# Seven-product W_o for two row blocks, two more nested down products, LayerNorm-2 statistics on ScalarE, and a new order table

## The chip, the cores and the metric

The kernel runs on one NeuronCore of one Trainium2 chip. The metric is the device time of one execution in microseconds (us), as the median of repeated runs. One execution was also taken with the hardware profiler. Its engines are called PE (TensorE), DVE (VectorE), ACT (ScalarE), POOL (GpSimd) and SP (SyncE, which here only issues DMAs).

## What is computed

A transformer block with adaptive LayerNorm: linear attention and a gated GELU feed-forward, on 2048 rows of 1024 features, F = 3584, in bfloat16.

```python
mod = (_silu(c) @ w_mod).reshape(c.shape[0], 6, 1, -1)   # sa, ca, ga, sb, cb, gb
h = _layernorm(x) * (1 + ca) + sa
x = x + ga * _A_ref(h, A_wqkv, A_wo)      # linear attention, then @ wo
h = _layernorm(x) * (1 + cb) + sb
x = x + gb * _B_ref(h, B_w_gate, B_w_up, B_w_down)
...
    qkv = (x @ wqkv) ...                  # 32 heads of 32
    pq, pk = phi(q), phi(k)
    kv = einsum('bhsd,bhse->bhde', pk, v); z = einsum('bhsd->bhd', pk)
    o = (pq @ kv) / (pq @ z + 1e-06)
    return o.reshape(B, S, D) @ wo
...
    return _gelu(x @ w_gate) * (x @ w_up) @ w_down
```

## The kernel before

**Tiling.** The 2048 rows are four blocks b of 512 rows (`TG`), two blocks make a group g of 1024 rows. `KD` = 8 chunks of 128 features, `KH` = 4 is half of them; `NPR` = 14 pairs of F chunks; `HB` = 256, `NW` = 512. SBUF is one tile `mem`, cut by hand: a ring or buffer is given by its offset in KB, and buffers of different phases share offsets. PSUM is eight banks, handed out by `Banks`.

**Phases, in program order.** `kvq_phase` (LayerNorm 1, then K, V and Q), `merge_phase` (the last Q products; the heads' KV matrices are multiplied into W_o, giving `Wp`, so that the attention output is one product of the normalised `pqT[b]` with `Wp`), `wo_phase`, then for each group `gate_up(g)` and `down_out(g)`.

**Half-size products.** Many of the big products are split into quadrants and done by seven half-size products instead of eight (Strassen's scheme in Winograd's form): DVE forms sums of the operands' quadrants (`h_sum`, `w_sum`, `h2_sums`, `wd_sums`), PE makes the seven products, and DVE and ACT combine them out of PSUM. `seven` (line 906) is the list of stages for row products: stage 1 copies P1 out by ACT, stages 2, 5 and 7 end in `comb` (a DVE addition of PSUM and a copied product), stage 6 in `direct`. Inside gate/up and down some of the seven are split in the same way once more; in the down stage these are called nested. There a plain product (`plain`, line 1649) is 4 row tiles x 14 matmuls of 512 columns, and a nested one (`nested`, line 1679) is 7 steps g1 to g7 of 2 x 7 matmuls of 256 columns.

**`wo_phase` (line 1371).** Sixteen row tiles tt of 128 rows, four to a block. `wo_tile` (line 1315) loads x, makes 2 x 8 matmuls of 512 columns into a pair of PSUM banks (line 1324), adds x by DVE and stores the sum x2 to DRAM from POOL's queue. `den_sums` and `den_mul` bring in the attention's denominators for the blocks to come. For the tiles of group 0 (tt < 8) LayerNorm 2 follows at once: `ln2_stats` takes the statistics by DVE (two `bn_stats` of 512 columns and a `bn_aggr`, lines 733 and 735) and the reciprocal root by ACT (Ln and Exp, lines 746 and 747); `ln2_xhat` normalises by DVE and stores to DRAM from POOL's queue; after the fourth and the eighth tile SP issues a DMA transpose that brings 512 rows back as h2 (`h2_load`, line 1259). `h2_mods` then scale and shift h2 chunk by chunk (ACT line 1302, DVE line 1304; the scale comes from line 1382), and `h2_steps` form the sums of its quadrants. The other eight tiles, tt 8 to 15, follow group 0's on PE while this happens. Group 1 is normalised later, by `late_norm` on ACT during `gate_up(0)`.

**`gate_up(g)` (line 1482).** 14 units n, alternately gate and up; each loads 1 MB of weights (line 1405), forms sums on DVE and makes seven products (line 1444; the nested ones at line 1455). `fill` is a list of DVE work (the next unit's sums; in group 0 also `wd_sums` for the down weights) that is recorded between the products.

**`down_out(g)` (line 1628).** Seven products named after their weights: b11, b21, t0, t1, b22, t2, t3. b21, t0 and b22 are nested (`NESTED`), the sums of their weights' quadrants lie in DRAM (`u_scr`, written by `wd_sums` in group 0); b11, t1, t2 and t3 are plain. `sub_sums` forms the nested products' sums of activations. b11's result P1 stays in PSUM banks 0 to 3, where t1, t2 and t3 add to it (`start=False`), and is copied to `p1v` by ACT (line 1754); the nested products use banks 4 to 7. `W_AT` gives the places of the weights: numbers n of 3.5 KB slots at 7 + 3.5 n KB, where gate/up's buffers also lie. `rest` loads x2, `finish` and the functions `..._out` apply the gate gb and add x2, `store` writes the output (in the last group from ACT's queue).

**Order.** No instruction is issued when the program calls it: all are recorded in a `Plan`. `order` (line 322) runs list schedules with estimated costs; PE's instructions keep the order of the program and the other engines' are sorted by due times (`aim` ties a load to a due time). `refine` (line 349) then applies a table of shifts to the sequence of each engine that has an entry:

```python
SHIFTS = {            # DVE, ACT, POOL, SP; "z5" stands for five zeros
...
        for e, text in SHIFTS.items():
...
            seqs[e] = [seqs[e][i + d] for i, d in enumerate(shifts)]
```

Each engine works through its own sequence in order. There is no entry for PE.

Of the kernel before, what the change touches and what calls it, by code (L numbers as in the profile page):

```python
# [19 lines left out]
SHIFTS = {  # L20
    "DVE": (
        "z1 7 8 -2 7 7 -2 -1 1 -7 4 -8 4 -8 -1 z1 -9 2 -1 -1 1 2 2 -3 2 4 1 1 2 2 2 2 2 -11 7 7 -11 16 16 -4 -2 -1 13 1 "
        "-5 -9 -3 -10 -2 -4 -2 -4 -2 -4 -3 -3 z2 2 z1 -2 3 -1 -1 -1 z2 1 -1 1 12 6 2 z1 12 -3 3 1 -9 -8 1 19 -2 18 -8 "
        "18 -3 z1 -3 -14 -1 5 1 1 -2 z1 1 1 1 6 17 -11 6 8 11 2 -4 -3 -2 z1 6 2 z1 -3 z1 3 3 -26 2 -35 18 -33 -1 9 6 6 "
        "-4 -2 5 6 35 -7 2 3 33 4 1 -9 8 1 1 2 28 2 3 -18 23 1 -6 z2 -28 -26 -24 -10 z1 -2 -5 -7 -2 -7 -2 -4 -7 7 -4 -6 "
        "-4 -4 -7 -4 -3 1 1 -2 4 1 3 4 2 3 -6 3 3 -6 2 -2 -11 2 -1 -1 3 44 -1 -3 1 -1 38 -5 -2 1 1 -4 1 -5 -5 1 -2 z1 "
        "-3 -7 -1 -3 3 -3 5 31 5 -3 5 -6 -9 -9 -5 5 -4 -9 -8 -5 2 4 -5 -5 -1 -1 -10 2 5 2 10 -3 -13 3 -13 4 -6 -5 3 3 3 "
        "4 -7 1 -10 -8 z1 10 3 5 z1 -4 6 6 9 -7 -4 4 -9 -4 z1 5 -9 -7 -2 -1 -1 z1 2 -1 -1 z1 2 z1 1 -3 z3 2 2 3 12 9 7 "
        "3 -1 z1 7 1 -11 -2 1 -13 -8 4 4 4 -15 -3 -2 -4 z2 5 2 -1 -3 z1 -3 4 1 3 -2 -4 -2 1 -1 3 4 5 1 -4 -4 -4 -1 1 1 "
        "1 -3 1 1 1 1 1 1 1 8 3 4 4 -1 -4 -1 -5 1 2 2 4 -19 1 3 3 4 -1 1 -9 2 2 -9 -2 2 5 6 1 -1 -4 -1 -7 2 -2 -1 3 1 "  # L30
        "-2 -2 2 -1 10 -2 z4 5 7 -2 -1 3 -2 3 -12 -7 2 2 -5 1 -3 3 z1 -2 2 2 6 2 -3 2 -2 -1 1 20 z1 1 3 4 z1 -4 z1 2 5 "
        "7 -7 12 -2 -1 -6 -4 -2 -2 2 -2 -2 4 7 -1 7 -36 -2 52 -1 -3 26 31 -4 z2 17 -15 -1 -8 -2 -5 40 -1 -5 11 25 -3 "
        "-15 -3 -3 -2 32 -13 35 -12 30 -16 -4 -4 z1 8 -3 -12 -19 -15 10 -5 -20 5 -4 -1 -5 -12 4 2 -11 -4 16 -11 -5 z1 "
        "-24 9 1 17 1 1 2 8 -26 -19 -13 3 29 z1 30 6 26 28 -17 -3 2 -51 1 -14 26 1 -7 -2 -1 24 -2 -14 -21 -2 13 13 -12 "
        "-7 -3 -5 -11 -23 37 38 17 -2 -13 10 -9 13 -13 -2 19 20 1 -1 9 -6 -6 -1 z1 -15 34 -25 16 -6 z2 15 9 -1 -1 -32 "
        "-10 -18 27 1 18 -46 25 19 20 -46 1 -12 -3 -22 -19 -2 37 -5 -3 -16 -2 -20 25 32 -8 -1 -1 -10 33 28 -16 -10 18 "
        "z1 18 36 -2 14 -18 -37 -13 -11 -1 -11 34 -6 -4 -7 -5 -4 -1 -5 12 -9 4 -7 3 -1 -22 11 29 -24 23 -44 4 z1 1 -1 "
        "-5 z1 7 -17 1 -13 -39 z1 -38 -3 -16 z1 4 2 30 20 21 -9 28 3 -16 -8 -4 -4 1 11 -14 4 4 20 17 3 10 12 4 -8 -12 2 "
        "-24 4 z1 7 -22 7 -14 12 -13 8 -22 2 -27 -23 4 6 8 -1 2 -28 6 4 5 -9 -1 7 -11 8 -6 8 9 -28 -2 11 8 12 -7 6 -10 "
        "12 6 21 7 -10 24 26 4 1 11 3 -9 -13 -7 z1 2 -24 9 16 18 24 6 8 17 -8 10 5 -6 10 -34 11 11 -13 -36 16 -20 -3 6 "  # L40
        "13 -17 -4 4 -3 10 3 1 10 2 -47 -25 9 -33 5 10 -6 13 15 -2 -33 1 6 9 27 1 8 10 -38 10 5 5 6 10 -11 5 -16 9 11 "
        "-8 7 z1 3 7 10 -16 10 -5 -4 10 10 7 11 11 11 11 12 -9 -44 -43 12 z2 -10 6 9 5 z1 1 7 3 -44 13 5 1 8 3 -53 6 "
        "-27 -3 6 -27 -3 5 -28 z1 -6 7 2 2 5 7 -5 -4 13 -3 7 -4 7 19 2 -20 18 -7 -7 -5 5 12 15 -8 3 -12 3 12 13 -1 -8 "
        "-1 -12 -15 10 -12 26 3 7 -13 6 11 -18 -7 -1 2 11 -16 -13 14 4 7 13 11 5 30 30 3 29 29 30 z1 4 8 -16 -10 1 1 2 "
        "4 -17 -2 z1 2 4 14 -2 -1 2 -2 -1 z1 -31 -1 9 -35 5 -4 -39 5 6 -7 z1 2 -56 12 12 z1 1 2 -58 11 -4 2 13 20 10 6 "
        "6 -7 -10 -55 -1 5 -11 z1 11 -7 2 -10 8 -17 4 -1 -18 8 -3 8 14 -10 -6 5 -11 -1 z1 8 2 8 19 -10 -1 6 7 -3 4 5 12 "
        "5 -11 10 -4 -20 2 8 11 -25 -15 5 6 -8 3 -8 6 -19 6 8 10 -1 9 10 -15 -11 9 -17 1 -4 7 13 6 1 13 -14 -8 4 -15 6 "
        "-14 12 -6 11 -1 5 6 -7 11 -17 -1 -3 -13 8 -3 10 -1 -1 z1 4 6 13 14 -21 -18 -1 15 4 -1 z1 2 8 -10 7 3 z1 7 1 4 "
        "-6 -12 4 4 -26 4 -25 -16 3 -1 5 2 4 7 10 8 -6 z1 1 -14 2 6 -1 -11 7 5 -12 -9 6 3 3 -3 6 3 1 12 1 4 11 -14 z1 2 "
        "6 3 8 z1 9 7 9 19 -24 -1 -23 6 4 -13 8 -18 -7 -6 5 -17 1 9 7 -5 1 -11 10 -8 z1 6 -10 7 10 -9 -7 -1 8 -4 7 -8 6 "  # L50
        "9 11 -6 -1 2 3 7 7 10 7 -12 -1 9 4 -7 4 -5 7 7 8 2 -30 6 z1 2 -5 7 7 2 3 12 12 -17 -4 -3 4 10 8 10 11 9 -5 -2 "
        "-5 8 8 -11 8 -48 -12 6 10 6 -2 11 12 -9 -58 -4 10 -3 3 6 -22 -2 5 5 -4 -2 -10 7 2 2 5 -2 7 -32 8 -18 2 -5 5 6 "
        "10 -4 5 14 -11 -5 3 -11 -7 9 10 2 7 9 -8 6 10 7 -10 6 -16 10 -8 11 -13 10 12 -15 9 4 -2 5 7 7 17 7 9 7 9 10 "
        "-13 2 -19 -2 -29 -15 -17 -15 -32 -3 8 5 8 -1 z1 -7 5 -4 6 6 6 -11 z1 5 -7 -10 6 -8 14 8 -3 8 -9 8 z1 -2 -7 -6 "
        "z1 6 -4 13 -2 z2 -10 2 9 -2 -19 -3 -2 -1 -1 5 -2 5 -7 6 7 -3 -3 z1 5 5 -5 5 -12 -3 -6 -3 -1 2 2 2 2 2 -5 -5 z3 "
        "6 2 2 -3 -3 -3 2 2 -1 -4 z6 "
    ),
    "ACT": (
        "z1 2 2 -2 -2 1 1 -2 z1 1 1 -2 2 z1 -2 3 4 4 4 4 4 5 3 4 4 -8 3 3 3 3 3 -16 3 1 3 1 2 2 -22 2 3 -1 2 2 -2 -26 "
        "z2 2 -1 1 2 -3 2 z1 -3 z1 2 z1 2 z1 -4 1 -1 z1 1 -1 z3 1 1 -2 z2 2 -1 -1 5 1 1 -3 -3 1 -2 z3 1 -1 z2 2 2 -2 -2 "  # L60
        "z3 2 -1 -1 2 z1 -2 z2 1 2 -2 -1 z1 2 -1 -1 1 -1 z4 2 -1 -1 z1 1 -1 z1 1 1 1 -3 z1 1 -1 z3 1 -1 1 1 1 -3 1 -1 1 "
        "-1 1 1 -2 z1 1 1 1 -3 z7 2 2 -2 -2 z6 2 -1 1 -2 3 z1 3 -3 z1 -3 z2 2 3 1 2 -3 1 -6 z1 29 30 -1 -1 -1 -1 -6 -1 "
        "-3 z1 1 -3 z2 1 3 -6 2 2 3 3 -5 -1 1 -7 1 -1 1 16 -2 2 2 -25 1 -4 1 18 1 -1 -4 -1 -1 -1 25 -2 -2 -1 4 z1 -3 2 "
        "-1 1 -6 8 z2 -43 z1 -2 -1 z1 1 1 1 -5 -17 z1 -2 1 -1 z1 1 1 -2 z1 2 z1 2 -3 -1 z5 1 -1 2 7 18 -3 2 2 3 -6 -4 2 "
        "-7 2 -2 1 2 2 2 2 -13 3 1 2 2 4 1 3 3 3 -2 3 1 2 2 2 -19 1 1 2 -26 1 1 -3 1 -1 z1 1 2 3 1 2 4 6 4 6 4 6 4 -5 4 "
        "4 5 3 -17 4 -17 3 z1 3 4 2 3 -2 3 5 3 -1 -23 3 3 z1 2 -5 1 2 -29 2 z1 1 2 2 3 -2 2 4 2 4 4 4 4 4 -16 3 3 3 4 "
        "-13 1 3 3 3 -15 -2 2 3 1 -17 1 1 1 -6 z1 1 -1 3 1 3 4 z1 3 5 6 4 -8 4 4 4 -3 3 3 3 4 -12 -19 z1 2 2 2 -2 2 3 1 "
        "3 1 2 2 -6 -24 2 -1 3 1 5 6 6 -4 -1 6 z1 5 5 8 8 8 9 9 -17 -13 -2 14 -3 7 -11 12 10 z1 12 9 9 12 2 -9 -6 -6 8 "
# [315 lines left out]
def kernel(  # L384
# [224 lines left out]
    for at_x2, n in ((191, 4), (176, 4), (136, 2)):  # L609
        x2_ring.slots += Ring(at_x2, [D], BF16, n).slots  # L610
# [1273 lines left out]
```

## Time and profile before

| | us |
|---|---|
| median of 3 runs (lowest, highest) | 743.55 (743.28, 744.94) |
| the profiled execution, its own time | 743.69 |
| its span, first to last instruction | 741.9 |

| stage | from | to | PE's work in it |
|---|---|---|---|
| LayerNorm 1, K, V, Q, merge | 0 | 187.9 | first rows transposed from 8.6, continuous from 16.9 |
| W_o | 187.9 | 245.1 | 256 matmuls of line 1324 |
| gate/up, group 0 | 245.1 | 411.9 | lines 1444 and 1455 |
| down, group 0 | 411.9 | 492.6 | lines 1656 and 1700 |
| gate/up, group 1 | 492.6 | 657.4 | lines 1444 and 1455 |
| down, group 1 | 657.4 | 738.5 | lines 1656 and 1700 |
| last additions and stores | 738.5 | 741.9 | none |

The stages are read from the chain of waits, which follows the work that ended last back to its start; 85% of the chain is PE. The whole program is one long row of matmuls with a start of 16.9 us and a tail of 3.4 us. How full the other engines are is read stage by stage, not from the sums over the span.

### The profile page before, as it was taken

Reading aid. Unit: us, or ns where it says so; the run is one execution under the profiler, and the core shown is the slowest. Engines: PE = TensorE matmul, PEld = TensorE weight load, DVE = VectorE, ACT = ScalarE, POOL = GpSimd, SP = SyncE. Lnnn points to the kernel's source line nnn. Section 1 sums busy time; section 2 is a strip of 40 time slices with the busy share of each in tenths; the row PEclk is TensorE's granted clock in tenths of the full one; section 3 lists DMA queues with packets and bytes.
Section 4 is the critical chain, followed back from the end, with each engine's and each line's share of the span. In section 5 each row is a group of like instructions: output and inputs, shape, how many; then the busy total and the mean of one; then the engine's idle time right before and its main releaser. Section 6 shows DMA issues by size and latency. Waiting matters only on the chain.

```text
span 741.9 us, 11731 instructions
## 1 busy us (share of the span) xinstructions
PE 726.5 (98%) x4242; PEld 396.1 (53%) x4242; DVE 626.3 (84%) x1386; ACT 422.8 (57%) x772; POOL 96.7 (13%) x171
## 2 busy tenths in 40 slices
PE   4999999999999999999999999999999999999997
PEld 2444445444444455555555586545555555548664
DVE  6899978778896999999997798977788799778784
ACT  2575675769412888999867550026776767732000
POOL 1345634100031011220200000001000000000000
PEclk9999999999999999999999999999999999999999
DMA  9998798897799737565775897545231322488643
GB/s 307 330 305 227 111 185 156 312 367 236 190 282 281 249 103 228 194 215 188 260 180 168 245 284 252 204 151 188 68 114 57 115 71 100 143 232 268 205 171 101
DMA packets 141723, 149.15 MB, mean 201 GB/s; under 512 B 33760, under 2 KB 121312, under 8 KB 140384
## 3 DMA queue, kind: packets, MB, share of 16 engines
q1 hardware_dynamic: 125408, 116.14, 51.4%
q0 software_dynamic: 13904, 30.15, 14.1%
q10 hardware_dynamic: 2352, 2.10, 0.9%
q8 instruction: 33, 0.54, 0.3%
q14 instruction: 26, 0.21, 0.1%
HBM read 116.00 MB, written 32.37 MB: 200 GB/s over the span
## 4 chain that ended last, share of the span: by engine, by line
PE 85%; DVE 7%; ACT 4%; issue 2%; DMA 1%; SPq 0%; DVEq 0%; ACTq 0%
PE psum L1444 26%; PE psum L1656 13%; PE psum L1455 9%; PE psum L958 8%; PE psum L1324 7%; PE psum L1028 7%; PE psum L1700 6%; DVE mem L655 5%; PE psum L1057 4%; PE psum L782 2%; ACT mem L903 2%; PE psum L1072 1%; DMA mem<-in_w_mod_dram 1%; DVE psum L655 1%; ACT mem L1281 1%
## 5 line engine op out<-in xcount | busy, mean ns | idle before, releaser
L655 DVE TENSOR_TENSOR mem<-mem 128x512 f16<-128x512 f16 (+13 forms) x753 | 336.6, 488 | 15.2 <-ACT mem L1302 4.1
L1444 PE MATMUL psum<-mem 128*128 128x512 f16 x1144 | 282.3, 379 | 0.6 <-ACT psum L1500 0.2
L903 ACT ACTIVATE mem<-psum 128x512 f32<-128x512 f32 (+3 forms) x310 | 161.0, 550 | 112.4 <-PE psum L1700 45.5
L655 DVE TENSOR_TENSOR mem<-psum,mem 128x512 f16<-128x512 f32 (+4 forms) x204 | 155.0, 765 | 36.8 <-PE psum L1656 10.1
L1444 PEld LDWEIGHTS <-mem 128*128 128x128 f16 (+1 forms) x1144 | 111.8, 98 | 91.4 <-issue 1.6
L1455 PE MATMUL psum<-mem 128*128 128x256 f16 x742 | 115.9, 272 | 0.7 <-DVE psum L655 0.7
L1455 PEld LDWEIGHTS <-mem 128*128 128x128 f16 (+1 forms) x742 | 72.5, 98 | 55.9 <-issue 2.7
L1656 PE MATMUL psum<-mem 128*128 128x512 f16 (+2 forms) x462 | 99.2, 373 | 0.5 <-DVE mem L655 0.5
L655 DVE TENSOR_TENSOR psum<-psum,mem 128x256 f32<-128x256 f32 x106 | 45.5, 430 | 32.4 <-ACT mem L903 31.6
L1656 PEld LDWEIGHTS <-mem 128*128 128x128 f16 x462 | 45.2, 98 | 49.9 <-issue 0.7
L1700 PE MATMUL psum<-mem 128*128 128x256 f16 (+1 forms) x588 | 66.3, 273 | 0.1
L958 PE MATMUL psum<-mem 128*128 128x512 f16 (+1 forms) x280 | 62.7, 379 | 0.0
L1700 PEld LDWEIGHTS <-mem 128*128 128x128 f16 x588 | 57.5, 98 | 9.5 <-issue 0.2
L1500 ACT ACTIVATE psum<-psum 128x512 f32<-128x512 f32 x56 | 32.6, 582 | 48.4 <-PE psum L1444 28.8
L1324 PE MATMUL psum<-mem 128*128 128x512 f16 x256 | 55.9, 379 | 0.0
L1028 PE MATMUL psum<-mem 128*128 128x512 f16 x224 | 51.0, 379 | 0.0
L958 PEld LDWEIGHTS <-mem 128*128 128x128 f16 x280 | 27.0, 98 | 31.5 <-DVE mem L879 0.5
L1324 PEld LDWEIGHTS <-mem 128*128 128x128 bf16 x256 | 24.8, 98 | 30.4 <-issue 0.4
L1028 PEld LDWEIGHTS <-mem 128*128 128x128 f16 (+1 forms) x224 | 21.6, 98 | 26.7 <-issue 1.6
L1527 ACT ACTIVATE mem<-mem 128x512 f16<-128x512 f16 x56 | 34.6, 627 | 2.0 <-DVE mem L655 2.0
L1517 ACT ACTIVATE mem<-psum 128x512 f16<-128x512 f32 x56 | 33.1, 600 | 2.1 <-PE psum L1444 2.0
L733 DVE BATCH_NORM_STATS2 mem<-mem 128x6 f32<-128x512 bf16 x48 | 31.2, 676 | 1.8 <-DMA mem<-in_A_x_dram 1.7
(126 smaller groups left out, 519.5 us busy)
## 6 DMA issues: line engine op xcount, KB each, us to landing
mem<-in_B_w_gate_dram SPq DMA_DIRECT2D x14, 1024.0 KB, 5.4
mem<-in_B_w_up_dram SPq DMA_DIRECT2D x14, 1024.0 KB, 5.6
mem<-in_w_mod_dram SPq DMA_DIRECT2D x24, 512.0 KB, 6.9
mem<-us SPq DMA_DIRECT2D x24, 448.0 KB, 6.2
mem<-ts SPq DMA_DIRECT2D x6, 1792.0 KB, 7.9
mem<-in_A_x_dram SPq DMA_DIRECT2D x32, 256.0 KB, 6.4
ts<-in_B_w_down_dram POOLq DMA_DIRECT2D x28, 256.0 KB, 6.5
us<-mem POOLq DMA_DIRECT2D x7, 768.0 KB, 4.8
```

Of the source, the lines that this page charges most:

```text
L655: ve.tensor_tensor(out=out, in0=a, in1=b, op=op)
L903: ac.activation(out=t, in_=ps, func=AF.Copy)
L958: te.matmul(ps, lhsT=A[:, k, i * P:(i + 1) * P], rhs=B[:, k, :], start=(start and k == 0), stop=(k == KH - 1), skip_group_check=True)
L1028: te.matmul(o, lhsT=W[:, k, (j0 + i) * P:(j0 + i + 1) * P], rhs=h_form(a, k), start=(start and k == 0), stop=(k == KH - 1), skip_group_che ...
L1324: te.matmul(psw[:, half, :], lhsT=pqT[b][:, g, tl * P:(tl + 1) * P], rhs=Wp[:, g, half * NW:(half + 1) * NW], start=(g == 0), stop=(g == K ...
L1444: te.matmul(ps, lhsT=a[:, k, e, :], rhs=b[:, k, :], start=(start and k == 0), stop=(k == KH - 1), skip_group_check=True)
L1455: te.matmul(ps, lhsT=self.x[a][:, k, :], rhs=self.y[y][:, k, :], start=(start and k == 0), stop=(k == KH // 2 - 1), skip_group_check=True)
L1500: ac.activation(out=z, in_=x, func=AF.Copy)
L1517: ac.activation(out=o, in_=ps, func=AF.Gelu_apprx_tanh)
L1527: ac.activation(out=o, in_=o, func=AF.Gelu_apprx_tanh)
L1656: te.matmul(psm[:, q, c], lhsT=A[:, i, q * P:(q + 1) * P], rhs=wt[:, i, c], start=(start and i == 0), stop=(i == NPR - 1), skip_group_chec ...
L1700: te.matmul(ps[:, q, :], lhsT=a[:, k, q * P:(q + 1) * P], rhs=y[:, k, :], start=(start and q == 0 and k == 0), stop=(k == NPR // 2 - 1), s ...
```

## The change

- **W_o of blocks 2 and 3.** Tiles 8 to 15 are replaced by `wo_stages(2)` and `wo_stages(3)`, each the stages of `seven` with `pqT[b]` and `Wp` split into quadrants. `w_sum` forms the sums over `Wp` (8 DVE instructions), `wo_sum` those over `pqT[b]` (4 per block). x is loaded in two loads of 512 KB per block, and x2 stored in two.
- **Place.** The two blocks' stages are interleaved, and the last two stages of block 3 are handed to `gate_up(0)`, which runs them behind its first eight matmuls.
- **LayerNorm-2 statistics of group 0** are taken by ACT: a copy and a square with accumulated sums, then Ln and Exp; DVE's `bn_stats` and `bn_aggr` go.
- **Down, group 1.** b11 and t2 become nested. Their weights' sums are formed during `gate_up(1)` by `wd_later` (7 chunks of 8 DVE additions of 256 columns, two loads of 256 KB, one store of 512 KB) and kept in `v_scr`. P1 is now put together by `p1_quads` and copied into banks 0 to 3 by ACT; t2's finish `c22_quads` also prepares what t3's finish `c21_last` adds. `W_AT` has new places for group 1.
- **Buffers** for all this are placed at offsets that other phases use.
- **The table** `SHIFTS` is new for every engine and has an entry for PE as well; its numbers are left out below.

```diff
 SHIFTS = {
+    "PE": (
...
-    for at_x2, n in ((191, 4), (176, 4), (136, 2)):
-        x2_ring.slots += Ring(at_x2, [D], BF16, n).slots
+    x2_ring.slots += Ring(136, [D], BF16, 2).slots
+    x2p_rings = {2: Ring(176, [2, D], BF16, 2), 3: Ring(191, [2, D], BF16, 2)}
+    WpT = [at(o, [KH, NW], F16) for o in (40, 152, 184)]
+    Sp = {b: [at(o + 2 * i, [KH, HB], BF16) for i in range(3)] for b, o in ((2, 34), (3, 44))}
+    wf_ring = Ring(140, [2, NW], FP32, 3)
...
+    LATER = ("b11", "t2")
...
+    def wd_later(c):
+
+        u, steps = wdw_ring(), []
+        for j, name in enumerate(LATER):
+            raw = wdv_rings[name]()
+            sy.dma_start(out=raw, in_=wd_full[name][:, 2 * c:2 * c + 2, :])
+            q11, q12, q21, q22 = (raw[:, e, h * HB:(h + 1) * HB] for e in range(2) for h in range(2))
+            o0, o1, o2, o3 = (u[:, j, f, :] for f in range(4))
+            steps += [(o0, q11, q12), (o2, q12, q22), (o1, o0, q22), (o3, o1, q21)]
+
+        def last():
+            tt_op(*steps[-1], ALU.add)
+            gp.dma_start(out=v_scr[:, c], in_=u)
 
         return [lambda st=st: tt_op(*st, ALU.add) for st in steps[:-1]] + [last]
...
-    def ln2_stats(x2, rstd_of):
-        mv = ln_stats(x2)
-        return mv, rstd_of(mv)
+    def ln2_stats(x2):
+        nmean, rstd = sum_ring(), rstd_ring()
+        ac.activation(out=junk2, in_=x2, func=AF.Copy, scale=-1.0 / D, accum_out=nmean)
+        ac.activation(out=junk2, in_=x2, func=AF.Square, bias=nmean, accum_out=rstd)
+        ac.activation(out=rstd, in_=rstd, func=AF.Ln, bias=eps5, scale=1.0 / D)
+        ac.activation(out=rstd, in_=rstd, func=AF.Exp, scale=-0.5)
+        return nmean, rstd
...
+    def wo_stages(b):
+
+        xs = {}
+        for r in range(2):
+            xs[r] = x2p_rings[b]()
+            o = b * TG + r * HB
+            plan.ahead = 36000
+            sy.dma_start(out=xs[r], in_=x_in[o:o + HB, :].rearrange("(q p) n -> p q n", p=P))
+            plan.ahead = 14000
...
+        def comb(ps, sb, row, col, parts=1):
+            t = wt_ring()
+            add_parts(t, ps, sb, parts)
+            tt_op(dst(row, col), t, dst(row, col), ALU.add)
+            if (row, col) == (0, 1):
+                store(0)
+
+        def direct(ps):
+            tt_op(dst(1, 0), ps, dst(1, 0), ALU.add)
+            store(1)
+
+        return seven(mm, comb, direct, *((QC, QD) if b == 2 else (QA, QB)), ring=wf_ring)
...
-        for tt in range(NTT):
+        for tt in range(2 * TT):
...
+            ln2_xhat(tt, xt, *ln2_stats(xt))
+            if tt in (2, 3, 4):
+                for half in range(2):
+                    w_sum(Wp, WpT, (0, 1, 3)[tt - 2], half)
+            if tt == 5:
+                for j in range(4):
+                    wo_sum(2, j)
+        for half in range(2):
+            w_sum(Wp, WpT, 2, half)
+        for j in range(4):
+            wo_sum(3, j)
+        s2, s3 = wo_stages(2), wo_stages(3)
+        stages = [*s2[:5], s3[0], s2[5], s3[1], s2[6], *s3[2:5]]
+        for i, f in enumerate(stages):
+            f()
...
+            for m in {3: h2_mods[0][0], 7: h2_mods[0][1], 9: h2_steps}.get(i, ()):
+                m()
...
+        return s3[5:]
...
-    def gate_up(g):
+    def gate_up(g, before=()):
...
         for e in range(2):
             mm_k(X[e], w["a11"], e, h["b11"], True)
             seed(Z[e], X[e])
+        for f in before:
+            f()
...
+            if g and n < NPR // 2:
+                fill += wd_later(n)
...
+        def p1_quads(r, c, ps, sb, op):
+            if sb is None:
+                ac.activation(out=quad(p1v, r, c), in_=ps, func=AF.Copy)
+            else:
+                tt_op(quad(p1v, r, c), ps, sb, op)
+            if (r, c) in ((1, 0), (0, 1)):
+                for q in (2 * r, 2 * r + 1):
+                    ac.activation(out=psm[:, q, :], in_=p1v[:, q, :], func=AF.Copy)
...
+        def c22_quads(x2, x1):
+            def out(r, c, ps, sb, op):
+                t, d = f16_pair(), quad(p5v, r, c)
+                if sb is not None:
+                    tt_op(sb, ps, sb, op)
+                    ps = sb
+                tt_op(t, d, ps, ALU.subtract)
+                tt_op(d, ps, gate2(0, c), ALU.mult)
+                tt_op(t, t, gate2(1, c), ALU.mult)
+                tt_op(quad(x2, r, c), t, quad(x2, r, c), ALU.add)
+                if (r, c) in ((1, 0), (0, 1)):
+                    store(x2, 1, 1, 2 * r, 2 * r + 2)
+                tt_op(d, d, quad(x1, r, c), ALU.add)
+            return out
...
+        def c21_last(xt):
+            def out(q, ps, c):
+                t = c0_ring()[:, c]
+                tt_op(t, ps, gbrow[:, c], ALU.mult)
+                tt_op(xt[:, q, c], t, p5v[:, q, c], ALU.add)
+                store(xt, 1, 0, q, q + 1, c)
+            return out
...
-        run(*plain("b11", A11, p1_out, True))
+        if last:
+            sub_sums(A11, sub_c[:3], sub_c[3], [slice(0, 4), slice(4, NPR // 2 - 1), slice(NPR // 2 - 1, NPR // 2)])
+            run(*nested("b11", A11, sub_c[:3], sub_c[3], p1_quads))
+        else:
+            run(*plain("b11", A11, p1_out, True))
...
+        if last:
+            sub_sums(A21, sub_a, None, [slice(0, NPR // 2)])
+            x2, x1 = rest(1, 1), rest(1, 0, last_x)
+            n7 = nested("t2", A21, sub_a, None, c22_quads(x2, x1))
+            run(n7[0], n3[5], n7[1], n3[6], *n7[2:])
+            run(*plain("t3", A22, c21_last(x1), False))
...
-    wo_phase(merge_phase(kvq_phase()))
-    gate_up(0)
+    gate_up(0, wo_phase(merge_phase(kvq_phase())))
```

## The prediction

> **What bounds the kernel now.** I read the head of the page first, then the chain of waits, then the busy time by stage, then the groups of VectorE (DVE) instructions with shapes kept apart. Durations come from the profiled execution: span 741.9 us, its own time 743.69, so 1.8 us lie around the span. The runs shown have a median of 743.55, 0.14 below the profiled one. I therefore take differences from the span and apply them to 743.55.
>
> ```profile
> span 741.9 us, 11731 instructions
> PE 726.5 (98%) x4242; PEld 396.1 (53%) x4242; DVE 626.3 (84%) x1386; ACT 422.8 (57%) x772; POOL 96.7 (13%) x171
> ```
>
> TensorE (PE) is busy nearly throughout, but "busy" contains modelled ends, so it has to be checked by counting. The chain of waits gives the pace of uninterrupted runs of matmuls:
>
> ```profile
> 192.66 17.37 PE psum L1324 x80
> 210.12 31.10 PE psum L1324 x144
> 241.65 3.45 PE psum L1324 x16
> ...
> 657.37 12.09 PE psum L1656 x56
> 669.46 18.34 PE psum L1700 x168
> ```
>
> Each line is start, length, line and count. A 512-column matmul takes 31.10/144 = 0.216 us, a 256-column one 18.34/168 = 0.109 us. With these two prices the W_o stage, gate/up and down are filled: gate/up of group 0 has 576 and 364 matmuls, 124.3 + 39.8 = 164.1 us of its 166.8; of group 1, 568 and 378, 163.9 of 164.8. Thus PE could lose at most 2.8 + 0.9 us of waiting there. A matmul removed between 17 us and 738 us shortens the kernel by its price, as long as nothing else becomes late. What could is DVE:
>
> ```profile
> 187.90:245.10 57.20, 57.20 (x279) 25.60 (x280) 48.20 (x80) 17.24 (x35) 11.50 (x21) 1.00 0.96 263
> 245.10:411.90 166.80, 165.75 (x942) 91.78 (x940) 156.29 (x401) 140.55 (x286) 21.43 (x34) 1.00 0.61 195
> 411.90:492.60 80.70, 80.63 (x520) 50.63 (x518) 68.87 (x124) 20.05 (x32) 2.87 (x4) 1.00 0.76 239
> 492.60:657.40 164.80, 164.54 (x948) 92.52 (x946) 132.16 (x327) 116.36 (x246) 2.84 (x4) 1.00 0.35 112
> 657.40:738.50 81.10, 80.58 (x532) 51.82 (x530) 62.06 (x106) 9.62 (x17) 0.00 (x0) 1.00 0.63 202
> ```
>
> Columns: stretch, length, then busy time of PE, weight loads, DVE, ScalarE (ACT), POOL, then clock, DMA share, GB/s. The rows are W_o, gate/up and down of group 0, gate/up and down of group 1. DVE is idle for 9.0, 10.5, 11.8, 32.6 and 19.0 us in them: everywhere second, but close.
>
> The Trainium skill's page "Perfetto Trace Analysis" (Identifying the Most-Contended Engine) says matmul busy time is a poor measure and weight-load busy time a good one. By that, 53% would leave TensorE nearly half free and cutting matmuls would bring nothing. The trace has a weight load at 98 ns under a 216 or a 109 ns pace, so its share follows the matmul's width; I go by the pace.
>
> **W_o by seven products.** Row blocks 2 and 3 were 8 tiles of 16 matmuls; now each block is 7 products x 2 halves x 4 = 56 instead of 64. 16 x 0.216 = **-3.45 us** of PE. Cover: DVE. It loses, for tiles 0 to 7, two statistics of 0.673 and one aggregate of 0.199 each (8 x 1.545 = -12.4), and 8 additions of 1.214 (-9.7). It gains 8 sums over Wp and 8 over the transposed rows at 0.69 (+11.0), and per block two combinations at 1.22 + 0.69, one at 0.69 + 0.69 + 0.69 and one direct 1.22, together 7.1 (+14.2). Net +3.1 us, half of it ahead of the path's need: during tiles 0 to 7, where DVE had been full, it is relieved by 12.4 and gets 6 sums over Wp and 4 over block 2 (6.9). ACT gains per tile a copy 1.064, a square 1.145 and two accumulator reads 0.207 + 0.194 (8 x 2.61 = 20.9) and 6.5 of PSUM copies; it is idle for 40 of 57 us there, so that costs nothing. The chain of one tile grows by 2.61 - 1.545 = 1.1 us. What queues behind the new ACT wait on the tile's addition is the next tile's statistics and the modulation of h2, nothing of PE's until block 2's first copy.
>
> **The junction into gate/up.** Tile 7 ends on PE at 210.12 + 32 x 0.216 = 217.0 in both kernels. Behind it lay 128 matmuls and two small ones (to 245.1); now 112. The first 8 gate products are placed ahead of the last 16 of W_o, so they start near 238.2 and not at 245.1; the first product that needs the second half of h2 moves from 246.8 to about 243.4, 3.4 us earlier. What it needs:
>
> ```profile
> 235.69 8.57 ACT L1302 ACTIVATE mem<-mem 128x512 f16<-128x512 f16 x12 [13.44 <-DVE mem L1382]
> ```
>
> ACT stood idle for 13.4 us before this modulation, for one 0.16 us DVE instruction placed late, so the first half's eight can move ahead. The second half follows tile 7: store on POOL at 223.3 to 224.4, second transpose out of SP by 233.6, and with DVE relieved this starts a little earlier, less the 1.1 us. I have room for about 3 us against 3.4 wanted. But 16 DVE sums (7.7 us) follow there without a gap. Bounds 0 (cover holds) and +3.45 (all that W_o gave is waited away); I take **+0.5**, nearer zero because both the relief and the idle 13.4 us are rows.
>
> **Two more nested products.** b11 and t2 of group 1: 56 matmuls of 0.216 = 12.09 become 98 of 0.109 = 10.70: 2 x 1.39 = **-2.78 us** of PE. The pace is that of the nested products already there. Added around it:
> Gate/up of group 1 gets 56 DVE sums of 0.286 (16.0 us, less where they overlap) into 32.6 us of idle, 14 loads on SP, which has one big load per unit there, and 7 stores on POOL (busy 2.84 of 164.8). 26.2 of the 32.6 us are waits of an in-order queue for ACT copies (the group that adds into PSUM, 54 times). If none of them could be filled, 6.4 us would be left and 16.0 - 6.4 = 9.6 us would come on top; if the queue is ordered so that a sum stands ahead of each such wait, nothing does. Bounds 0 and +9.6; I take 0, since nothing needs these sums before 657 and DVE's order is made anew with them in it.
> Down of group 1 gets on DVE the sums over A11 (4 x (0.69 + 0.42 + 0.29) = 5.6, of which only the last 4 x 0.29 must wait for gate/up's end), over A21 (4 x 1.09 = 4.4), three combinations of P1 (2.1), a longer finish for t2 (per quadrant 2.9, and 0.69 in three: 13.7 for 6.1, +7.6), and 0.27 in each last addition (+1.1): 20.8 us by durations. With the 62.1 there now that is 82.9 in a stage of 81.1 - 2.8 = 78.3: 4.6 too many. It fits only if the 4.4 of A11 run in gate/up, which had 16 us left after the 56 sums, and because instructions overlap a little (two of 0.69 take 1.28). SP issues 14 loads for 2, some 1.2 us each, and DMA carries 2.7 MB more beside 16.6; the first seven can go before 657, where the DMA share is 0.57. Bounds 0 and the overflow worked out under the rivals; I take **+0.5**, nearer zero because 8.7 us of DVE's idle time lie between 720 and 738.5, where half of the longer t2 finish falls.
> The tail keeps its form; its last addition reads f32 instead of f16: 0.42 for 0.29, **+0.1**.
>
> **The shift table.** All queues are reordered, PE's for the first time. The gain is bounded by PE's waits: 3.7 us in gate/up and about 1 us at 16 us; the loss by group 0's gate/up, which loses 2.8 under the table of now. I take **-0.8**.
>
> Sum: -3.45 + 0.5 - 2.78 + 0.5 + 0.1 - 0.8 = -5.9 us. 743.55 - 5.9 = **737.6 us**, span near 736.0.
>
> **Rivals.**
> *Junction wait.* The transpose and the modulation can't come earlier, PE waits out W_o's gain. For it: tile 7 ends no earlier, DMA share is 0.96 there. Against: the rows above. 743.55 - 2.78 = 740.8 (the other small terms cancel).
> The Trainium skill's page "TensorE: Matmul & The Clock Gate" (The HAM clock gate) says an idle window of about 3.4 us halves TensorE's clock until it has worked as long again; by this the rival would cost an estimated 1.7 us more, 742.5. The trace has 512-column matmuls at 634 ns around 9 to 15 us, after the idle start, and 379 later, though the clock column shows 1.00.
> *DVE becomes the bound in the last down stage* (slower). Place: 657 to 720, where DVE idles 3.1 + 7.2 = 10.3 us. If the table lets nothing run early, 5.6 + 2.1 + 4.4 and half of the 7.6, 15.9 us, fall into it: 5.6 us too many, and the t3 product ends 5.6 us later than before. 743.55 - 3.45 + 5.6 = 745.7. It decides the sign once the overflow passes 3.45. Against: A11's parts are complete well before 657, and its buffers are free.
> *Nothing is felt*: PE isn't the bound, each removed matmul returns as a wait; 743.5. The counting speaks against it.
> *More than the sum*: the new matmul order also recovers gate/up's waits: 743.55 - 6.2 - 2.8 = 734.5. DVE's 10.5 us idle in group 0's gate/up leave little for it.
>
> **How the numbers follow.** A measurement of this kernel tells about 0.2% (1.5 us) from no change. Forecast 0.66 (its own range 735.6 to 739.2), more 0.08, junction 0.12, nothing felt 0.03, DVE-bound 0.11. Faster 0.66 + 0.08 + 0.12 = 0.86, same 0.03, slower 0.11. The range 735.0 to 741.5 takes in the forecast, the junction case and part of the better one, leaving out about 0.19.
>
> **What would show it.** W_o's seven products as 112 matmuls at 0.216, from the first to gate/up's first inner product 3.5 us shorter; no PE gap over 0.5 us between 236 and 250; LN2's squares on ACT with DVE's statistics gone from W_o. Gate/up of group 1 still 164 to 165 us with DVE near 148 busy. Down of group 1 near 78.5 us from its first matmul to its last, DVE near 80 busy including its early parts. I am wrong if PE's idle time grows by over 2 us in one place, or if down of group 1 takes over 80 us.

## The result, and the profile after

| | before | after |
|---|---|---|
| median (lowest, highest) | 743.87 (743.28, 744.94), 4 runs | 754.72 (753.99, 755.68), 4 runs |
| the profiled execution, its own time | 743.69 | 754.85 |
| its span | 741.9 | 753.1 |

The ratio is 1.0145, interval [1.0127, 1.0163]: 10.85 us slower, where 5.9 us faster was forecast. The head of the page after:

```profile
span 753.1 us, 12047 instructions
PE 735.8 (98%) x4297; PEld 402.6 (53%) x4310; DVE 659.3 (88%) x1472; ACT 452.2 (60%) x819; POOL 99.7 (13%) x174
```

PE is 98% busy and its weight loads 53%, as before. Neither figure shows that some work on PE became dearer. The busy time by stage after, in the columns of the prediction's table (the first row is W_o, from its first matmul to gate/up's first; then gate/up and down of group 0, gate/up and down of group 1):

```profile
200.60:256.60 56.00, 54.80 (x264) 23.02 (x263) 46.93 (x73) 39.07 (x70) 7.94 (x15) 1.00 0.80 228
256.60:423.00 166.40, 166.30 (x944) 91.95 (x943) 158.71 (x408) 143.05 (x291) 24.27 (x37) 1.00 0.70 216
423.00:506.00 83.00, 82.89 (x529) 51.79 (x530) 68.41 (x120) 21.11 (x35) 3.53 (x5) 1.00 0.75 232
506.00:670.00 164.00, 163.82 (x948) 92.39 (x947) 149.83 (x400) 117.30 (x247) 6.00 (x11) 1.00 0.50 160
670.00:749.00 79.00, 78.73 (x613) 59.55 (x611) 74.44 (x124) 13.34 (x23) 0.00 (x0) 1.00 0.81 235
```

From gate/up's start to the last stage's end it takes 749.0 - 256.6 = 492.4 us, before 738.5 - 245.1 = 493.4, though the last 16 products of W_o (3.5 us) now lie in it; the edges of single stages are less sharp, since products of neighbouring stages alternate. But W_o begins at 200.6 and not at 187.9: **12.7 us are lost before W_o starts**, in K, V and Q, where the change had altered nothing but the order.

What differs there is seen on PE's timeline. Columns: start, length, line, operation, weights (128*32: 128 rows, 32 columns), count. First before, then after:

```profile
32.37 3.62 PE L1057 MATMUL psum<-mem 128*128 128x512 bf16 x16
35.92 1.05 PE L727 MATMUL psum<-mem 128*32 128x512 bf16 x16
36.90 13.99 PE L1057 MATMUL psum<-mem 128*128 128x512 bf16 x64
```

```profile
38.48 0.39 PE L840 MATMUL psum<-mem 128*32 128x512 bf16 x1
38.80 0.39 PE L1171 MATMUL psum<-mem 128*128 128x512 bf16 x1
39.12 0.40 PE L840 MATMUL psum<-mem 128*32 128x512 bf16 x2
39.44 1.04 PE L1171 MATMUL psum<-mem 128*128 128x512 bf16 x4
40.41 0.40 PE L840 MATMUL psum<-mem 128*32 128x512 bf16 x3
40.74 0.60 PE L1171 MATMUL psum<-mem 128*128 128x512 bf16 x2
41.28 0.61 PE L840 MATMUL psum<-mem 128*32 128x512 bf16 x8
```

Before, sixteen products with weights 32 columns wide ("narrow" below: sums for the modulation, and the denominators) follow each other: the next full product begins 36.90 - 35.92 = 0.98 us later, 61 ns for each. After, the new order has them in ones, twos and threes among full products. The starts tell what that costs: from the single narrow product at 38.48 to the end of the full one behind it (next start 39.12) it is 0.64 us; less 0.216 for the full one, **0.42 us for one narrow product**. The three at 40.41 cost about as much (41.28 - 40.41 - 2 x 0.216 = 0.44). No engine is named as the releaser: nobody is waited for, so no view of waits shows this, and the modelled ends overlap so that PE looks busy.

Counted from the starts, behind 21 us of each trace, as the time from the full product ahead of a run of narrow ones to the full one behind it, less one full pace:

| narrow products in the run | time | runs before | runs after |
|---|---|---|---|
| 1 to 4 | 0.41 to 0.44 us (one of 0.63) | 0 | 36 |
| 5 to 8 | 0.63 to 0.65 | 0 | 6 |
| 10 | 0.85 | 0 | 1 |
| 13 to 16 | 1.07 (one of 1.31) | 6 | 1 |
| 32 | 1.94 | 1 | 0 |
| all 128 | | 8.61 us in 7 runs | 21.15 us in 44 runs |

So a run costs about 0.205 us once, and 0.2155 us, one full product's pace, for every four begun. The starts inside the sixteen at 35.92 show the fours: four products start within 0.01 us, and the next four 0.21 us later. The difference is **+12.5 us**: 37 runs more at 0.205 make 7.6, 23 more groups of four (55 for 32) at 0.2155 make 5.0. (13 of this trace's 4310 matmul records are missing; the single 0.63 for a run of three can be one of them.)

### The profile page after: what moved, and what is told of

Read it like the earlier page. It is cut to its first block, busy times and chain, and to the rows that moved or that the text cites. A ratio compares the mean times of both kernels' runs of the same rounds, so it can differ in the third digit from the quotient of the medians.

```text
span 753.1 us, 12047 instructions
## 1 busy us (share of the span) xinstructions
PE 735.8 (98%) x4297; PEld 402.6 (53%) x4310; DVE 659.3 (88%) x1472; ACT 452.2 (60%) x819; POOL 99.7 (13%) x174
## 4 chain that ended last, share of the span: by engine, by line
PE 91%; DVE 7%; issue 1%; DMA 1%; SPq 0%; ACT 0%; DVEq 0%; ACTq 0%
PE psum L1637 32%; PE psum L1898 11%; PE psum L1648 11%; PE psum L1072 8%; PE psum L1853 6%; PE psum L1142 6%; DVE mem L768 6%; PE psum L1458 4%; PE psum L1171 3%; PE psum L1522 2%; PE psum L895 2%; PE psum L785 1%; PE psum L1186 1%; PE psum L840 1%; DMA mem<-in_A_x_dram 1%
## 5 line engine op out<-in xcount | busy, mean ns | idle before, releaser
L768 DVE TENSOR_TENSOR mem<-mem 128x256 f16<-128x256 f16 (+12 forms) x857 | 378.4, 484 | 13.2 <-PE psum L840 2.3
L1637 PE MATMUL psum<-mem 128*128 128x512 f16 x1144 | 300.6, 379 | 0.1
L1016 ACT ACTIVATE mem<-psum 128x512 f32<-128x512 f32 (+3 forms) x320 | 169.8, 557 | 137.6 <-PE psum L1898 46.4
L768 DVE TENSOR_TENSOR mem<-psum,mem 128x512 f16<-128x512 f32 (+5 forms) x213 | 159.2, 755 | 42.1 <-ACT mem L1016 9.4
L1648 PE MATMUL psum<-mem 128*128 128x256 f16 x742 | 138.7, 272 | 0.2 <-ACT psum L1654 0.2
L1898 PE MATMUL psum<-mem 128*128 128x256 f16 (+1 forms) x784 | 96.6, 273 | 0.0
L1898 PEld LDWEIGHTS <-mem 128*128 128x128 f16 x784 | 76.5, 98 | 18.3 <-DVE mem L768 0.3
L1853 PE MATMUL psum<-mem 128*128 128x512 f16 (+2 forms) x348 | 81.9, 371 | 0.3 <-DVE mem L768 0.2
L1072 PE MATMUL psum<-mem 128*128 128x512 f16 (+1 forms) x272 | 66.1, 379 | 0.3
L1142 PE MATMUL psum<-mem 128*128 128x512 f16 x224 | 55.6, 380 | 0.6 <-DVE mem L768 0.6
L768 DVE TENSOR_TENSOR psum<-psum,mem 128x256 f32<-128x256 f32 x106 | 45.2, 427 | 12.5 <-ACT mem L1016 11.0
L1853 PEld LDWEIGHTS <-mem 128*128 128x128 f16 x350 | 34.2, 98 | 31.2 <-issue 0.4
L1072 PEld LDWEIGHTS <-mem 128*128 128x128 f16 x280 | 26.7, 98 | 29.2 <-DVE mem L992 0.8
L1171 PE MATMUL psum<-mem 128*128 128x512 bf16 x125 | 32.2, 380 | 0.1
L1458 PE MATMUL psum<-mem 128*128 128x512 f16 x128 | 29.1, 380 | 0.0
L1522 PE MATMUL psum<-mem 128*128 128x512 f16 x112 | 26.4, 379 | 1.2 <-DVE mem L768 0.8
```

The costliest lines, as they stand in the source:

```text
L768: ve.tensor_tensor(out=out, in0=a, in1=b, op=op)
L1016: ac.activation(out=t, in_=ps, func=AF.Copy)
L1072: te.matmul(ps, lhsT=A[:, k, i * P:(i + 1) * P], rhs=B[:, k, :], start=(start and k == 0), stop=(k == KH - 1), skip_group_check=True)
L1142: te.matmul(o, lhsT=W[:, k, (j0 + i) * P:(j0 + i + 1) * P], rhs=h_form(a, k), start=(start and k == 0), stop=(k == KH - 1), skip_group_che ...
L1171: te.matmul(ps, lhsT=hr1[b][:, k, tl * P:(tl + 1) * P], rhs=Wk[:, k, n * NW:(n + 1) * NW], start=(k == 0), stop=(k == KD - 1))
L1458: te.matmul(psw[:, half, :], lhsT=pqT[b][:, g, tl * P:(tl + 1) * P], rhs=Wp[:, g, half * NW:(half + 1) * NW], start=(g == 0), stop=(g == K ...
```

## The experiments

**Narrow products put back together.** After the table, every run of narrow products that stands unbroken in the program is put at the place of its last one; all other orders stay.

```diff
             seqs[e] = [seqs[e][i + d] for i, d in enumerate(shifts)]
+        seqs["PE"] = self.regroup(seqs["PE"])
...
+    def regroup(self, seq):
+        narrow = lambda op: op.args[0].ap[0][1] <= 32 if op.fn == "matmul" and op.args else False
+        pe = [op for op in self.ops if op.eng == "PE"]
...
+        last = {}
+        for op in seq:
+            last[run[op.n]] = max(last.get(run[op.n], 0), at[op.n])
+        return sorted(seq, key=lambda op: (last[run[op.n]] if narrow(op) else at[op.n], op.n if narrow(op) else 0))
```

> The changed kernel; in PE's sequence each run of 32-column-wide products (the modulation sums and denominators, which the new matmul order broke into 44 runs behind 21 us) is put back together at the place of its last one. Theory N (a narrow product alone among full-width ones costs some 0.42 us, four together the same): 44 runs take 21.15 us in the changed kernel against 8.61 in 7 runs before, so 12.5 us come back, and about 1 us of the start: 741 to 743. Rival D (DVE is the bound in the last down stage, or the wait at the junction): the time stays at 750 or more.

Measured: 743.04 us (741.82 to 745.34, 10 runs) beside 743.81; ratio 0.9992 [0.9982, 1.0002]. With this one edit 754.72 - 743.04 = 11.7 us are gone: all of the loss. The interval does not tell this kernel from before. 743.04 is 0.04 us above the range that was expected, and the rival (750 or more) falls. Head and timeline of this kernel:

```profile
span 740.0 us, 12059 instructions
PE 722.5 (98%) x4310; PEld 401.3 (54%) x4310; DVE 658.6 (89%) x1472; ACT 451.9 (61%) x819; POOL 99.6 (13%) x174
```

```profile
35.57 1.05 PE L855 MATMUL psum<-mem 128*32 128x512 bf16 x16
36.55 10.53 PE L1186 MATMUL psum<-mem 128*128 128x512 bf16 x48
```

The sixteen take 0.98 us again, and PE's busy time falls from 735.8 to 722.5 with the same products: what the page calls busy was the cost of the alternation.

**The order of before for PE, the new tables for the rest.** The table's entry for PE alone is taken out.

```diff
 SHIFTS = {
-    "PE": (
...
     "DVE": (
```

> The changed kernel without the table's entry for PE: matmuls in program order, the other four tables as they are. Theory N: narrow runs are whole again, so at least 10 us come back unless the other tables, made for the other matmul order, now make PE wait: 740 to 747. Rival D: 750 or more, since DVE's work is the same.

Measured: 778.82 us, ratio 1.0469 [1.0453, 1.0484]. The 740 to 747 is missed, and the time lies in the rival's range, but not for its reason. The narrow products stand in seven runs again and take 8.7 us, as they do in before; other waits cover that up. The excess (start to start on PE, less the pace of 0.216, 0.109 or, for a narrow product, 0.061 us, summed over a stage) is 17.5 us in gate/up of group 0, where after has 1.7, and 11.8 us in that of group 1 for 1.5: the other queues' tables were made for PE's new order, and in the old one PE waits for DVE and ACT, mostly in gate/up (the longest group, 9.0 us in 15 waits, is for DVE). The entries of these tables can't be judged one at a time, and the time of this run says nothing on the narrow products.

**The cost by itself, in the kernel before.** 32 narrow products that stand ahead of W_o are set singly behind W_o's first 32 products, then by fours behind the first eight.

```diff
+        seqs["PE"] = self.scatter(seqs["PE"], 1)
...
+    def scatter(self, seq, each):
...
+        for op in seq:
+            if op.n in ids:
+                continue
+            out.append(op)
+            if op.line == 1343 and left:
+                out += left[:each]
+                del left[:each]
```

> The kernel before; the 32 narrow products of the last modulation set, which stand in one run ahead of W_o, are set one by one behind the first 32 matmuls of W_o; nothing else is moved. Theory N: 32 single runs of 0.418 us less one of 1.935: 11 us slower, all of it in W_o's first 40 matmuls. Rival M (the cost that the program's own plan uses, narrow product = a fixed share of a full one wherever it stands): 0.

> As the scatter by one, but four narrow products behind each of eight matmuls. Theory N: 8 runs of 0.434 less 1.935: 1.5 us slower. If instead the cost goes by the number of narrow products between full ones: as much as the scatter by one; rival M: 0.

Measured once each, beside 743.81: 755.87 singly (+12.1) and 745.09 by fours (+1.3). By the table above, 32 runs of one are 32 x 0.42 = 13.4 for 1.94, +11.5, and eight runs of four 3.4 for 1.94, +1.4. A single time 0.3 us above the slowest of before (744.78) would be weak evidence for the fours, but the starts agree: the 128 narrow products take 20.8 us in all with the 32 set singly, 9.9 with them by fours, and 8.6 in before. The timeline of the first:

```profile
187.17 0.39 PE L1343 MATMUL psum<-mem 128*128 128x512 f16 x1
187.49 0.39 PE L691 MATMUL psum<-mem 128*32 128x512 bf16 x1
187.81 0.39 PE L1343 MATMUL psum<-mem 128*128 128x512 f16 x1
188.13 0.39 PE L691 MATMUL psum<-mem 128*32 128x512 bf16 x1
```

Each change costs: a pair takes 0.64 us where a full product takes 0.216. This shows the cause in a kernel that has nothing else of the change.

The weight loads (PEld) of the same stretch show more than the products do:

```profile
187.16 0.10 PEld L1343 LDWEIGHTS <-mem 128*128 128x128 bf16 x1 [0.23 <-issue]
187.48 0.09 PEld L691 LDWEIGHTS <-mem 128*32 128x32 bf16 x1 [0.23 <-issue]
187.80 0.10 PEld L1343 LDWEIGHTS <-mem 128*128 128x128 bf16 x1 [0.23 <-issue]
188.12 0.09 PEld L691 LDWEIGHTS <-mem 128*32 128x32 bf16 x1 [0.23 <-issue]
```

Each load starts with its own product. Counted over this trace, the load of a full product behind another full one starts 0.214 us ahead of its product (the median of 3918), about when the product in front starts; at the 74 changes of width it starts at most 0.005 us ahead. A load takes 0.09 to 0.10 us, and a run, with its two changes, costs 0.205 us once. So each change costs about one weight load that is not hidden. Why the load comes so late there, no run shows.

**The parts without any table.** To price W_o and the nested products apart, four kernels run in the list schedule's own order: before, after, before with the W_o part, and before with the two nested products.

```diff
-SHIFTS = {
...
+SHIFTS = {}
```

> The kernel before with an empty shift table: only the list schedule orders DVE, ACT, POOL and SP. It is the base for the three runs beside it. Slower than 743.8; by how much, neither theory says.

> The changed kernel with an empty shift table, so its narrow products are whole. If the parts of the change are worth what was predicted (6.2 us of matmuls less about 1 us of waits): 4 to 6 us under the base without a table. If the changed parts make PE wait for DVE (rival D): level with it or slower, whatever the table.

> Only the W_o part (seven products for blocks 2 and 3, statistics on ScalarE, its place in gate/up), empty table. Theory: 3.45 us of matmuls less; if its products wait for DVE's sums as in the regrouped run, 2 to 3 us of that are waited away in W_o and the gain is about 1.

> Only b11 and t2 of group 1 nested, with the sums of their weights in gate/up of group 1; empty table. Predicted: 2.78 us of matmuls less and 0.5 of waits, so 2.3 under the base. Rival D (DVE the bound in the last down stage): 2 us or more over it, with the gap behind 657.

Measured (once each): 755.56, 761.77, 767.55 and 750.71. The whole change is 6.2 us slower here, where 4 to 6 less was expected, although its narrow products stand in seven runs. The nested products alone bring 4.85 us. Their stage, by first and last matmul, goes from 81.0 to 80.1, its waits from 1.1 to 2.5; the rest comes from a list schedule that falls out differently in K, V, Q and gate/up of group 0 (excess 13.9 there for 18.4; in each of these four traces 12 to 14 records of matmuls are missing, which can put up to 3 us too much into such a count). W_o alone loses 12.0, where a gain of about 1 was expected: in its stage the excess is 14.4 us for 0.2, and 14.0 with the whole change. The busy time of the W_o-only kernel in five stretches:

```profile
219.40:224.20 4.80, 0.40 (x2) 0.00 (x0) 2.20 (x4) 4.05 (x10) 1.08 (x2) 1.00 0.50 187
224.30:231.00 6.70, 5.68 (x14) 2.05 (x15) 4.75 (x8) 1.02 (x1) 0.54 (x1) 0.50 0.49 126
231.10:241.30 10.20, 6.55 (x30) 2.66 (x29) 6.96 (x13) 5.03 (x7) 0.00 (x0) 1.00 1.13 269
241.40:244.70 3.30, 3.30 (x9) 1.18 (x8) 2.93 (x5) 0.81 (x1) 0.00 (x0) 0.50 1.09 369
244.80:250.00 5.20, 5.20 (x25) 2.35 (x24) 3.88 (x5) 5.20 (x9) 0.72 (x1) 1.00 1.10 362
```

PE waits there twice for DVE, 5.5 us up to 225.3 and 3.7 us up to 240.6. From 224.3 on, as the first wait ends, the granted clock (the number behind POOL's) is 0.50 for 6.8 us, and from 241.3 on, just behind the second, for 3.4 us. So this change does have a place where W_o's gain can turn into a wait, inside W_o, and the table of after keeps it small. These four kernels differ in the whole order, so their differences are not clean prices of the parts.

**Where the narrow products are best put.** At the place of the first of each run, and of the middle one.

```diff
-            last[run[op.n]] = max(last.get(run[op.n], 0), at[op.n])
+            last[run[op.n]] = min(last.get(run[op.n], at[op.n]), at[op.n])
```

```diff
-            last[run[op.n]] = max(last.get(run[op.n], 0), at[op.n])
+            last.setdefault(run[op.n], []).append(at[op.n])
+        last = {r: p[len(p) // 2] + 0.5 for r, p in last.items()}
```

> As the regrouped run, but each narrow run stands at the place of its first product instead of its last, so what follows from it (denominators, modulation) starts earlier. Theory N: the narrow products cost the same as regrouped, so 741 to 744; if the 0.9 us waits at 162 and 187 us come from late narrow runs, 1 to 2 us under the regrouped run; if their weights have not landed at the earlier place, slower than it.

> Each narrow run at the place of its middle product. Theory N: within 2 us of the regrouped run, between it and the run with the first place.

Measured: 753.87, ratio 1.0139 [1.0122, 1.0155], and 742.59 (740.70 to 745.02, 10 runs) beside 743.94, ratio 0.9976 [0.9961, 0.9992]. The middle gives the one order of the whole change whose time lies clear of before's, 0.24% under it; it is 0.45 us under the run with the last places and not, as expected, between that and the first. The first place is too early, in part because the weights have not landed, as the third case had it:

```profile
23.55 0.40 PE L855 MATMUL psum<-mem 128*32 128x512 bf16 x4
25.57 0.40 PE L855 MATMUL psum<-mem 128*32 128x512 bf16 x4 [1.62 <-DMA mem<-in_w_mod_dram]
26.92 0.40 PE L855 MATMUL psum<-mem 128*32 128x512 bf16 x4 [0.96 <-DMA mem<-in_w_mod_dram]
28.28 0.40 PE L855 MATMUL psum<-mem 128*32 128x512 bf16 x4 [0.96 <-DMA mem<-in_w_mod_dram]
```

Each four waits for its own piece of the modulation's weights. This run of sixteen takes 5.16 us for 1.07, and behind its waits the granted clock is 0.50 from 29.5 to 32.9 us, by estimate 1.7 us more (half of the 3.4). A second run of sixteen, near 200 us, takes 4.97, since it waits 1.9 and 1.5 us for DVE. Together that is 9.7 of the 10.8 us between 753.87 and 743.04. The late weights may be why an order made by trial would spread these products, each as early as its data: by the plan's cost model (lines 213 and 214 of before: a product with at most 32 columns of weights costs the time of a full one divided by 3.5, wherever it stands) spreading is free. That this is how the table came to be is argued, not shown.

**What is left in W_o.** With the narrow products together, PE still loses 2.3 us in W_o where before lost 0.4. The waits there, of the kernel with the runs at their last place (columns: who waits, for whom, us in total, times, longest):

```profile
PE psum L1537 <- DVE mem L783: 0.8, 2, 0.6
PE psum L1473 <- DVE mem L783: 0.7, 1, 0.7
PE psum L1537 <- ACT mem L1031: 0.3, 1, 0.3
```

Two runs ask what DVE is late with. First the 16 sums of W_o go:

```diff
+                A2 = {"s1": q[:, hi, be], "s2": q[:, lo, al], "s4": q[:, hi, al]}.get(a, A)
+                B2 = {"t1": Wp[:, 0:KH, 0:NW], "t2": Wp[:, KH:KD, 0:NW], "t4": Wp[:, KH:KD, NW:D],
+                      "t3": Wp[:, 0:KH, NW:D]}.get(w, B)
+                plan.ops[-1].kw.update(lhsT=A2[:, k, i * P:(i + 1) * P], rhs=B2[:, k, :])
...
+                plan.left_out |= {op.n for op in plan.ops[-2:]}
```

> The regrouped run without the 16 DVE sums of W_o's operands (8 over Wp, 8 over the rows); the seven products read unsummed quadrants instead, so the output is not the reference's. PE's work and order are the same. Theory W (the seven products of W_o wait for these sums, which come behind the denominators' way through DRAM): PE's waits in W_o fall from 2.3 us to under 0.8 and the time by 1.5 to 2.5 us. Rival: the waits stay, since the denominators themselves are what is late, and at most 0.5 us is gained.

Measured: 743.45 us, ratio 0.9989 [0.9979, 0.9999]; excess in W_o 2.1 us, the same waits. So the sums are not what is late. Then the products' dependence on the denominators goes too:

```diff
-                q = pqT[b]
-                A2 = {"s1": q[:, hi, be], "s2": q[:, lo, al], "s4": q[:, hi, al]}.get(a, A)
+                q = pqT[b - 2]
+                A2 = {"a11": q[:, lo, al], "a12": q[:, hi, al], "a22": q[:, hi, be], "s3": q[:, lo, be],
+                      "s1": q[:, hi, be], "s2": q[:, lo, al], "s4": q[:, hi, al]}[a]
```

> The kernel of e11 with one more part left out: W_o's products for row blocks 2 and 3 read the rows of blocks 0 and 1, which were divided by their denominators long before, so nothing on TensorE in this stage waits for the denominators of blocks 2 and 3 any longer (they are still formed, stored, loaded and multiplied in). The queues keep their order. Theory D (what is late in W_o are these denominators): the excess over the pace in W_o falls from 2.1 us to under 0.6, as in the kernel before, and the time is 1 to 2 us under e11, 741.5 to 742.5 beside its 743.45. Rival (the waits come from PSUM tiles set free late by DVE, whose queue still holds the multiplications by the denominators, or from anything else in the stage): the excess stays at 1.5 us or more and the time within 0.7 us of e11.

Measured: 742.95 us, ratio 0.9989 [0.9978, 1.0001]; excess in W_o 1.6 us, 0.5 less than without the sums alone. Counted from the starts, waits of 0.81 and 0.36 us near 223 have become one of 0.66 at 225.6; one of 0.49 us at 240 is as it was. By the bounds set the rival holds: by these two traces the denominators are about a quarter of it, while the medians (743.45 and 742.95) lie within each other's spread. What else DVE and ACT finish late there (the combinations of PSUM tiles are what is left) stays open.

## Why the prediction was wrong

**The step that failed is "The shift table".** It reads: "The gain is bounded by PE's waits: 3.7 us in gate/up and about 1 us at 16 us; the loss by group 0's gate/up, which loses 2.8 under the table of now." It was taken at -0.8 and came out at +12.5 for the narrow products alone. A new order was priced by the waits that it can mend or make; the bound of the loss was a wait of another table in another stage, and bounds nothing here. That an instruction's duration can depend on its neighbours was not considered, although the chain of waits before had the row: sixteen narrow products of 512 columns in 0.98 us, 61 ns each, beside 216 ns for a full one. A product of 512 columns can't stream in 61 ns by the pace of the others, so several must run at once, and whatever breaks the run up takes that away. Before has the price too: a run of sixteen takes 1.07 us and one of 32 takes 1.94, which makes 0.2175 for each four more and 0.20 for the run itself. The diff said that PE is ordered anew, the table's entries were in it, and the places of 128 narrow products could have been worked out from them.

The Trainium skill's page "TensorEngine Tiling (Array Packing)" bears on both halves of this: under Theoretical Speedup, that a small dimension of up to 32 allows up to four times the speed, and under Key Properties, that a change of the tiling mode drains TensorE. The traces agree with the first (four in 0.2155 us). For the second they give a price, 0.205 us for each run; that it is a drain they don't show, only that the weight load at a change is not ahead of its product. The page has no price, but it would have been a reason to look for the one that before's own runs hold, and with 37 runs more that price turns the sign of this step.

The account of the span, before to after: products saved -3.45 - 2.78, narrow products +12.5, other waits of PE +3.7 (as the kernel with the runs together has them: K, V, Q 2.4 and W_o 1.9 more, gate/up and down together 0.6 less), tail +0.8; together +10.8, measured 753.1 - 741.9 = +11.2, with 0.4 left open.

**The other steps:**
- *What bounds the kernel*: right. With the same products on PE, only their order decides; regrouping alone moves 11.7 us.
- *W_o by seven products*: the 112 products run at their pace. Chain of after:

```profile
208.02 9.17 PE psum L1458 x42
...
236.22 10.59 PE psum L1522 x48
```

  9.17 / 42 is 0.218; 10.59 / 48 is 0.221, with waits in it. LN2 moved to ACT as said, ACT staying at 39 of 56 us. But of the 3.45 us saved, 1.9 come back as waits, so the term is nearer -1.6, and its cover, DVE, is not as loose as "relieved by 12.4".
- *The junction into gate/up*, +0.5: nothing over 0.5 us is lost at the place that was feared. The largest gap on PE between 236 and 250 is 0.48 us in the kernel with the runs together; there it is copies of PSUM by ACT that are late, not the modulation of h2. The waits come earlier in W_o, from 220.5 and 222.6, where none was looked for.
- *Two more nested products*, -2.78: right. Gate/up of group 1 takes 164.0 us with DVE at 149.8 (said: 164 to 165, near 148), down of group 1 79.0 us with DVE at 74.4 (said: 78.5, near 80). PE has 0.6 us of excess there for 0.7 before, so DVE did not become the bound; that rival fell.
- *The tail*, +0.1: +0.8. In after's timeline, the last lines of DVE:

```profile
747.24 1.69 PE L1853 MATMUL psum<-mem 128*128 128x256 f16 x14 [0.17 <-DVE mem L768]
747.70 0.68 DVE L768 TENSOR_TENSOR mem<-psum,mem 128x512 f16<-128x512 f32 x1
748.30 1.02 DVE L768 TENSOR_TENSOR mem<-mem 128x256 bf16<-128x256 f16 x2
749.43 0.42 DVE L768 TENSOR_TENSOR mem<-psum,mem 128x256 f16<-128x256 f32 x1
749.89 0.43 DVE L768 TENSOR_TENSOR mem<-mem 128x256 bf16<-128x256 f16 x1
```

  The f32 addition is 0.43 for 0.29, as priced. But DVE is still at the quarter ahead (1.02 us from 748.30) when the last matmul, begun at 748.66, is done; the last addition out of PSUM starts 0.77 us behind that matmul's start. Before it was 0.31 (738.56 - 738.25), DVE waiting for PE:

```profile
738.56 0.42 DVE L655 TENSOR_TENSOR mem<-psum,mem 128x256 f16<-128x256 f32 x1 [1.45 <-PE psum L1656]
739.02 0.29 DVE L655 TENSOR_TENSOR mem<-mem 128x256 bf16<-128x256 f16 x1
```

  The term counted the last instruction and not the queue in front of it.
- *The rivals*: none happened. The one on the slower side named the wrong engine; the clock rule beside the junction (the Trainium skill's page "TensorE: Matmul & The Clock Gate", The HAM clock gate) bears on the W_o-only kernel, where the granted clock is 0.50 for 6.8 and 3.4 us behind waits of 5.5 and 3.7 us. The trace agrees with it there. But in the same trace it is 0.50 for 3.4 us behind a wait of only 2.2 us, which ends at 305.9, and with the first places it is so behind three waits of 1.62, 0.96 and 0.96 us: shorter waits than the page's window of about 3.4 us were enough, and the measurement decides. After has no such wait and a clock of 0.999.

Without the narrow products' cost the forecast would still have been some 5 us too low: 742.59 and 743.04 for 737.6. In their profiled executions (741.15 and 741.82) that is the waits in K, V, Q and W_o and the tail, as in the account. Their medians lie 1.2 to 1.4 us above those executions, with a wider scatter than before's; why stays open.

## What to carry to other kernels

When an order changes, ask not only who will wait, but whether any instruction is cheap only because of its neighbours: a duration per instruction far under what its shape takes elsewhere is the sign. Keep products with 32-column weights in unbroken runs of a multiple of four, at a place where all that they read has landed; a cost model that prices them alike everywhere will scatter them, and a busy share of 98% hides it, so count starts against the pace. The tables of shifts here were made together and can't be changed singly: with one entry taken out the time was 778.8 us.

## What the runs showed that was not expected

- A narrow product of 512 columns costs 61 ns in a run of 16 or 32, and 0.42 us alone among full ones, nearly seven times as much and twice a full product; one to four cost the same.
- Alternating full products of different lines, widths (512 and 256 columns) and PSUM tiles shows no cost: in gate/up of after the two widths alternate, near its start in pieces of one to eleven, and at its 712 changes between them the median start to start is the pace within 0.001 us. PE's excess in the two gate/up stages together is 3.3 us, where before had 3.7.
- PE's busy time rose by 9.3 us (726.5 to 735.8) although the change takes work from it, while the durations shown for one narrow product hardly moved: the median over the 48 modulation products of one line (L727 before, L840 after) is 0.384 us before, where they stand in runs, and 0.390 after. Starts, not durations, tell the two apart.
- A weight load takes 0.09 to 0.10 us whether it is hidden or not; what tells is when it starts: 0.214 us ahead of its product inside a run, with its product at a change of width.
